# Attention, soft mixture of experts and a Mish layer in one kernel: the small products that build the next slice of the combined weight, placed one unit earlier

## The chip, the cores and the metric

The kernel runs on one core of one Trainium2 chip. The metric is the device time of one execution in microseconds (us). A core has five engines, each with its own instruction queue: TensorE (PE, with its weight loads shown apart as PEld), VectorE (DVE), ScalarE (ACT), GpSimd (POOL) and SyncE (SP, which issues the DMAs here).

## The reference

Three layers follow each other. `phi`, `w1`, `w2`, `w_in` and `w_out` are parameters, and all is in 32-bit floating point.

```python
q_rot, k_rot = (rotate(q), rotate(k))                 # (4, 8, 576, 64)
attn = softmax(1/sqrt(D) * q_rot @ k_rot.T)
x = (attn @ v) laid out as (2304, 512)

logits = x @ phi                                      # 8 experts x 4 slots
d = softmax(logits, axis=0); slot_input = (d.T @ x).reshape(E, 4, 512)
slot_out[e] = np.maximum(slot_input[e] @ w1[e], 0.0) @ w2[e]
x = softmax(logits, axis=1) @ slot_out                # rank 32

h = x @ w_in                                          # (2304, 2048)
g = h * np.tanh(softplus(h))                          # mish
return g @ w_out                                      # (2304, 512)
```

## The kernel before

The kernel has three stages: attention (to about 390 us of the span), the expert products, and from about 439 us on the Mish layer. The change lies in the Mish layer alone.

**The Mish layer.** Since x is the softmax `c` (2304 x 32) times `slot_out` (32 x 512), h = c @ (slot_out @ w_in). The kernel first builds the combined weight W = slot_out @ w_in in `wst` (2048 columns), and then takes c.T (`ct`) through it. Work goes in *units*: unit u is a block of 256 tokens (index i) against a slice j of 256 of the 2048 columns. There are 9 token blocks in three groups g of three, and 8 slices. In each group, for each slice j in turn, come three units, one per token block; these three are a *step* below. The first group (units 0 to 23) also builds W and the parts of w_out; the other two groups reuse them.

For a unit, `mish(u)` (L1000 to L1009) does two matmuls of 256 columns into the PSUM tile `hp`, the Mish activation on ACT into `gg`, and a rounded copy `gh`. `rest(u)` (L1015) takes the rest `gl` = gg - gh on DVE. `second(u)` (L1034) does twelve matmuls of 512 columns into the output tiles `o_ps`: gh times `wo_h`, gh times `wo_l`, and, last, gl times `wo_h`. It runs one unit behind: PE does hp of unit u, then the second product of unit u - 1.

**Inner products.** Slice j of W comes from two small products. `inner_a(j)` (L977, L978) does four matmuls of `s_t` with a block of w_in into the PSUM tile `m_wp`, which ACT copies. `inner_b(j)` (L983 to L986) does one matmul of that copy into `m_w`; ACT copies it into `wst`, and DVE takes the rest of rows 64 to 127 there by a subtraction. hp of slice j reads the result of that subtraction. `hp`, `m_wp` and `m_w` share two PSUM buffers.

```python
def inner_b(j):
    ps = ps_p.tile([128, 256], F32, tag="p", name="m_w")
    pin(nc.tensor.matmul(ps, lhsT=rr, rhs=wps[j % 2], start=True, stop=True))
    dst = wst[:, j * 256:(j + 1) * 256]
    pin(nc.scalar.copy(dst, ps))
    pin(nc.vector.tensor_tensor(out=dst[64:128], in0=ps[64:128], in1=dst[64:128].bitcast(F32), op=ALU.subtract))
```

**Chunks of w_out.** w_out comes in 16 chunks of 128 rows, each as a rounded part `wo_h` and a rest `wo_l`; slice j needs chunks 2j and 2j + 1. Chunks 0 to 3 were prepared earlier and lie in `wo_l`; `parts_of(c)` splits one, with a copy on ACT (L940) and a subtraction on DVE (L941). Chunks 4 to 15 are loaded raw and converted in small steps: two scale operations on ACT (L871, L872), five on DVE (L874, L876, L879, L881, L883), then a copy on ACT (L885) and a last subtraction on DVE (L887). `convert(n)` emits the next n DVE steps of this stream, with the ACT operations among them; a raw load (L863) goes out from within it. Each unit calls it with 3, the first unit of a step with 4.

**Order.** `pin` keeps all these instructions in the order of the code, so each engine's queue is the order in which the loop over units calls these functions:

```python
for u in range(len(units) + 2):
    ...
        mish(u)
        if u == 0:
            convert(3)
            idle(5)
        else:
            if u in (1, 2):
                parts_of(u + 1)
            if g == 0 or u == NG * GR:
                rest(u - 1)
                convert(3 + (i == 0))
            ...
    if u >= lag and u != NG * GR:
        second(u - lag)
    ...
    if g == 0 and j + 1 < NG:
        if i == 1:
            inner_a(j + 1)
        elif i == 2:
            inner_b(j + 1)
```

So within step j, m_wp of the next slice follows the second product in unit i = 1, and m_w follows it in unit i = 2, right ahead of hp of the next step. Ahead of the loop stand `inner_a(0)`, `inner_b(0)`, `parts_of(0)` and `parts_of(1)`; `idle(n)` puts n matmuls of no use (`warm`) on PE. In the trace `room` is the name of several work tiles (gg, raw chunks, copies of m_wp).

Of the kernel before, what the change touches and what calls it, by code (L numbers as in the profile page):

```python
# [42 lines left out]
def kernel(  # L43
# [78 lines left out]
    def fetch(key, behind=False):  # L122
        m, e, hf = key
        t = parts[key][0]
        if m == 3:
            lds = [(t.rearrange("p (c f) -> p c f", c=KDM), scr_in[e])]
        else:
            w = (w1, w2)[m - 1]
            n = w.shape[1] // 2
            lds = [(t.rearrange("p (c f) -> p c f", c=n // 128),  # L130
                    w[e, hf * n:(hf + 1) * n, :].rearrange("(c p) f -> p c f", p=128))]
            if (m, e // 4, hf) == (2, E // 4 - 1, 1):

                final.append(lds.pop())
                if len(final) == 4:
                    lds = [(o[:, c], i[:, c]) for c in range(n // 128) for o, i in final]
        for out, in_ in lds:
            ld = nc.sync.dma_start(out=out, in_=in_)
            if behind:
                tc.keep_in_program_order(ld)  # L140
# [724 lines left out]
    def cv(c, k):  # L865

        lo, hi = words(raws[c % 4])
        w = ws3[c % 3]
        wb, sf = w.bitcast(U32), sg.bitcast(F32)
        if k == "S":  # L870
            pin(nc.scalar.activation(out=hi.bitcast(F32), in_=hi.bitcast(F32), func=AF.Copy, scale=2.0 ** -112))  # L871
            pin(nc.scalar.activation(out=lo.bitcast(F32), in_=lo, func=AF.Copy, scale=2.0 ** -52))  # L872
        elif k == 1:
            pin(nc.vector.tensor_scalar(out=sg, in0=hi, scalar1=0x80000000, scalar2=None, op0=ALU.bitwise_and))  # L874
        elif k == 2:
            pin(nc.vector.scalar_tensor_tensor(out=wb, in0=hi, scalar=3, in1=sg, op0=ALU.logical_shift_left,  # L876
                                               op1=ALU.bitwise_or))
        elif k == 3:
            pin(nc.vector.tensor_scalar(out=sg, in0=wb, scalar1=0xFF800000, scalar2=None, op0=ALU.bitwise_and))  # L879
        elif k == 4:  # L880
            pin(nc.vector.tensor_tensor(out=sf, in0=sf, in1=lo.bitcast(F32), op=ALU.mult))  # L881
        elif k == 5:
            pin(nc.vector.tensor_tensor(out=w, in0=w, in1=sf, op=ALU.add))  # L883
        elif k == "H":
            pin(nc.scalar.copy(wo_h[c], w))  # L885
        else:
            pin(nc.vector.tensor_tensor(out=wo_l[c], in0=w, in1=wo_h[c].bitcast(F32), op=ALU.subtract))  # L887
# [49 lines left out]
    def parts_of(c):  # L937

        x = wo_l[c].bitcast(F32)
        pin(nc.scalar.copy(wo_h[c], x))  # L940
        pin(nc.vector.tensor_tensor(out=wo_l[c], in0=x, in1=wo_h[c].bitcast(F32), op=ALU.subtract))  # L941
# [21 lines left out]
    def convert(n):  # L963
        while n:
            x = next(steps2, None)
            if x is None:
                return
            cv(*x)
            n -= x[1] not in ("S", "H")

    def inner_a(j):

        fb, o = divmod(j * 256, 512)
        wi = parts[3, fb, 0][0].rearrange("p (c f) -> p c f", c=KDM)[:, :, o:o + 256]
        ps = ps_p.tile([128, 256], F32, tag="p", name="m_wp")
        for c in range(KDM):
            pin(nc.tensor.matmul(ps[32 * c:32 * c + 32, :], lhsT=s_t[:, c, :], rhs=wi[:, c, :], start=True, stop=True))  # L977
        pin(nc.scalar.copy(wps[j % 2], ps))  # L978
# [8 lines that stand above are left out]
# [8 lines left out]
    def mish(u):  # L995
        i, j = units[u]
        hp = ps_p.tile([128, 2, 256], F32, tag="p", name="hp")
        for x in range(2):
            f = 2 * j + x
            pin(nc.tensor.matmul(hp[:, x, :], lhsT=wst[:, f * 128:(f + 1) * 128],  # L1000
                                 rhs=ct[:, i * 256:(i + 1) * 256],
                                 start=True, stop=True))
        hp = hp.rearrange("p a n -> p (a n)")
        gg = ggs[u % 3]
        gh = p6.tile([128, 512], F32R, tag="gh", name="gh", bufs=LOOK + 1)
        gl = p6.tile([128, 512], F32R, tag="gl", name="gl", bufs=LOOK + 1)
        pin(nc.scalar.activation(out=gg, in_=hp, func=AF.Mish))  # L1007

        pin((nc.scalar.copy if 0 < u < NG * GR else nc.vector.tensor_copy)(gh, gg))  # L1009
        gs[u] = gh, gl, gg  # L1010

    def rest(u):

        gh, gl, gg = gs[u]
        pin(nc.vector.tensor_tensor(out=gl, in0=gg, in1=gh.bitcast(F32), op=ALU.subtract))  # L1015
        gs[u] = gh, gl
# [3 lines left out]
    def second(u):  # L1020
        i, j = units[u]
        gh, gl = gs.pop(u)
        todo = [(n, x, k) for n in range(2) for x in range(2) for k in range(3)]
        if u < NG * GR:

            todo.sort(key=lambda y: y[2] == 2)
        if j == 0:
            for n in range(2):
                ops[i, n] = ps_o.tile([128, DM], F32, tag="o", name="o_ps")
        for at, (n, x, k) in enumerate(todo):  # L1030
            g_, w_ = ((gh, wo_h), (gh, wo_l), (gl, wo_h))[k]
            f = 2 * j + x
            cols = slice(x * 256 + n * 128, x * 256 + n * 128 + 128)
            pin(nc.tensor.matmul(ops[i, n], lhsT=g_[:, cols], rhs=w_[f], start=(j == 0 and (x, k) == (0, 0)),  # L1034
                                 stop=(j == NG - 1 and all(y[0] != n for y in todo[at + 1:]))))
            if j == NG - 1 and all(y[0] != n for y in todo[at + 1:]):
                ob = obs[(2 * i + n) % 4]
                pin((nc.scalar.copy if n else nc.vector.tensor_copy)(ob, ops.pop((i, n))))
                store(2 * i + n, ob)
# [17 lines left out]
    def idle(n):  # L1057

        warm(ps_o, "o", n)
# [8 lines left out]
    for u in range(len(units) + 2):  # L1068

        lag = 1 if u < NG * GR else 2  # L1070
        if u < len(units):
            g, j = units[u][0] // GR, units[u][1]
            i = units[u][0] % GR
            mish(u)
            if u == 0:
                convert(3)
                idle(5)
            else:
                if u in (1, 2):
                    parts_of(u + 1)  # L1080
                if g == 0 or u == NG * GR:
                    rest(u - 1)
                    convert(3 + (i == 0))
                if g:
                    rest(u)
        else:
            g = None
        if u >= lag and u != NG * GR:
            second(u - lag)
        if g == 0 and i == 2 and j in (0, 2):  # L1090
            fetch((3, 2 + j // 2, 0), behind=True)
        if g == 0 and j + 1 < NG:
            if i == 1:
                inner_a(j + 1)
            elif i == 2:
                inner_b(j + 1)
    ring.close()

# [49 lines left out]
```

## Time and profile before

| | us |
|---|---|
| median of 3 runs (lowest to highest) | 682.52 (682.22 to 687.17) |
| the profiled execution | 684.97 |
| its span, first to last instruction | 683.2 |
| PE busy in the span | 629.7 (92%) |
| DVE busy | 408.0 (60%) |
| ACT busy | 337.2 (49%) |
| POOL busy | 216.9 (32%) |

The profile is one execution, taken by the hardware profiler. A timeline row gives the start from the span's beginning, the duration, the engine, the line of the code, the operation, what it writes and reads, and how many were merged (x2); in square brackets stands how long the engine had been idle before it and what ended that. Matmuls overlap each other, so the difference of two starts says more than a duration. Engines run side by side: idle time of one that is not the slowest costs nothing.

### The profile page before, as it was taken

Reading aid. Unit: us, or ns where it says so; the run is one execution under the profiler, and the core shown is the slowest. Engines: PE = TensorE matmul, PEld = TensorE weight load, DVE = VectorE, ACT = ScalarE, POOL = GpSimd, SP = SyncE. Lnnn points to the kernel's source line nnn. Section 1 sums busy time; section 2 is a strip of 40 time slices with the busy share of each in tenths; the row PEclk is TensorE's granted clock in tenths of the full one; section 3 lists DMA queues with packets and bytes.
Section 4 is the critical chain, followed back from the end, with each engine's and each line's share of the span. In section 5 each row is a group of like instructions: output and inputs, shape, how many; then the busy total and the mean of one; then the engine's idle time right before and its main releaser. Section 6 shows DMA issues by size and latency. Waiting matters only on the chain.

```text
span 683.2 us, 11115 instructions
## 1 busy us (share of the span) xinstructions
PE 629.7 (92%) x4034; PEld 463.2 (68%) x4034; DVE 408.0 (60%) x824; ACT 337.2 (49%) x757; POOL 216.9 (32%) x263
## 2 busy tenths in 40 slices
PE   1698899987899999999999898988989999999997
PEld 1566677665676677677667664456767888888885
DVE  6677688787687865656565533276766533343332
ACT  2565676684687656655566312265655311221121
POOL 6668768754968545424300010000000000000000
PEclk9999999999999999999999999999999999999999
DMA  8778589777886975436559579943200300030003
GB/s 258 185 181 223 167 269 265 227 208 226 198 245 210 280 201 144 106 96 167 133 182 321 191 248 379 402 165 138 78 32 2 92 1 0 1 93 0 1 1 93
DMA packets 59607, 109.43 MB, mean 160 GB/s; under 512 B 12832, under 2 KB 25248, under 8 KB 59040
## 3 DMA queue, kind: packets, MB, share of 16 engines
q1 hardware_dynamic: 59552, 108.72, 53.4%
q8 instruction: 32, 0.52, 0.3%
q14 instruction: 23, 0.19, 0.1%
HBM read 70.25 MB, written 9.96 MB: 117 GB/s over the span
## 4 chain that ended last, share of the span: by engine, by line
PE 76%; DMA 9%; DVE 6%; ACT 3%; POOL 2%; issue 1%; SPq 1%; ACTq 0%; DVEq 0%; POOLq 0%
PE o_ps L1034 29%; PE m_av L429 13%; PE t L374 7%; PE s L333 5%; PE s L335 4%; DMA w<-in_moe_w_in_dram 3%; PE hp L1000 3%; PE so_ps L896 2%; PE s L353 2%; DMA w<-in_moe_w_dram 2%; PE m_lg L455 1%; DVE nmax L361 1%; PE warm L553 1%; ACT P L367 1%; PE tk L388 1%
## 5 line engine op out<-in xcount | busy, mean ns | idle before, releaser
L361 DVE TENSOR_REDUCE nmax<-s 128x1 f32<-128x576 f32 x144 | 108.0, 752 | 64.6 <-PE s L335 41.6
L367 ACT ACTIVATE P<-s,nmax 128x576 f32<-128x576 f32 x144 | 107.2, 745 | 37.9 <-DVE nmax L361 26.1
L1034 PE MATMUL o_ps<-wo_h,gh 128*128 128x512 f32 x288 | 113.1, 393 | 0.1
L1034 PE MATMUL o_ps<-wo_l,gh 128*128 128x512 f32 x288 | 113.0, 392 | 0.0
L1034 PE MATMUL o_ps<-wo_h,gl 128*128 128x512 f32 x288 | 100.9, 391 | 2.3 <-DVE gl L1015 2.3
L1007 ACT ACTIVATE room<-hp 128x512 f32<-128x512 f32 x72 | 43.0, 599 | 112.2 <-PE hp L1000 107.5
L333 PE MATMUL s<-qk_st 128*128 128x288 f32 x256 | 86.0, 351 | 11.9 <-ACT P L367 6.0
L374 PE MATMUL t<-cs,P 128*128 128x128 f32 x512 | 79.4, 283 | 4.8 <-ACT P L367 2.7
L410 ACT COPY PT<-t 128x512 f32<-128x512 f32 x92 | 53.5, 586 | 49.5 <-PE t L374 48.8
L429 PE MATMUL m_av<-PT,w 128*64 128x320 f32 (+1 forms) x384 | 73.9, 422 | 3.2 <-DVE PT L413 1.9
L374 PEld LDWEIGHTS t<-cs,P 128*128 128x128 f32 x512 | 59.9, 143 | 22.1 <-issue 10.2
L335 PE MATMUL s<-k_st,qk_st 128*128 128x288 f32 x256 | 74.1, 303 | 0.0
L333 PEld LDWEIGHTS s<-qk_st 128*128 128x128 f32 x256 | 50.1, 196 | 32.0 <-ACT P L367 10.4
L1009 DVE CAST gh<-room 128x512 fp32r<-128x512 f32 x49 | 20.9, 427 | 79.1 <-ACT room L1007 78.9
L1034 PEld LDWEIGHTS o_ps<-wo_h,gl 128*128 128x128 f32 x288 | 53.9, 188 | 14.9 <-DVE gl L1015 3.5
L231 POOL TENSOR_TENSOR w<-w,cs 128x512 f32<-128x512 f32 x34 | 45.2, 1330 | 55.0 <-PE m_k L285 45.1
L1034 PEld LDWEIGHTS o_ps<-wo_h,gh 128*128 128x128 f32 x288 | 54.1, 188 | 9.6 <-DVE gh L1009 0.3
L1034 PEld LDWEIGHTS o_ps<-wo_l,gh 128*128 128x128 f32 x288 | 54.4, 189 | 8.9
L1015 DVE TENSOR_TENSOR gl<-room,gh 128x512 fp32r<-128x512 f32 x72 | 49.6, 690 | 5.0 <-DVE gh L1009 0.5
L335 PEld LDWEIGHTS s<-k_st,qk_st 128*128 128x128 f32 x256 | 50.5, 197 | 0.0
L228 POOL TENSOR_TENSOR w<-w,cs 128x512 f32<-128x512 f32 x34 | 45.1, 1326 | 9.0 <-DMA w<-in_k_dram 4.8
L429 PEld LDWEIGHTS m_av<-PT,w 128*64 128x64 f32 x384 | 26.6, 136 | 24.3 <-issue 9.3
(175 smaller groups left out, 1014.1 us busy)
## 6 DMA issues: line engine op xcount, KB each, us to landing
w<-in_moe_w_dram SPq DMA_DIRECT2D x28, 1024.0 KB, 7.5
w<-in_moe_w_in_dram SPq DMA_DIRECT2D x16, 512.0 KB, 7.7
qk_st<-parth SPq DMA_DIRECT2D x46, 144.0 KB, 3.2
qk_st<-partl SPq DMA_DIRECT2D x46, 144.0 KB, 3.3
room<-in_moe_w_out_dram SPq DMA_DIRECT2D x12, 512.0 KB, 3.5
w<-in_q_dram SPq DMA_DIRECT2D x16, 256.0 KB, 5.5
w<-in_k_dram SPq DMA_DIRECT2D x16, 256.0 KB, 5.1
w<-in_moe_w_dram SPq DMA_DIRECT2D x16, 256.0 KB, 5.9
```

The costliest lines, as they stand in the source:

```text
L228: eng.tensor_tensor(out=tb, in0=src, in1=sin.to_broadcast([128, n, w]), op=ALU.mult)
L231: eng.tensor_tensor(out=dst, in0=sv, in1=cv, op=ALU.mult)
L333: nc.tensor.matmul(s[:, half, 0:288], lhsT=st[:, qc:qc + 128], rhs=st[:, KC + o:KC + o + 288], start=first, stop=False)
L335: nc.tensor.matmul(s[:, half, 0:288], lhsT=st[:, qc:qc + 128], rhs=k2_st[p % 2][:, o:o + 288], start=False, stop=last)
L361: nc.vector.tensor_reduce(out=stat[p][0][:, i:i + 1], in_=s[:, :, 0:288], axis=AX.XY, op=ALU.max, negate=True)
L367: nc.scalar.activation(out=P[p, t][:, h * S:(h + 1) * S].rearrange("p (a b) -> p a b", a=2), in_=s[:, :, 0:288], func=AF.Exp, bias=stat[p] ...
L374: nc.tensor.transpose(ps[:, j, :], P[p, t][:, blk * 128:(blk + 1) * 128], ident)
L410: nc.scalar.copy(dst, src)
L429: nc.tensor.matmul(ps[o:o + 64, :], lhsT=lhsT, rhs=rhs, start=(c == 0), stop=(c == 4))
L1007: pin(nc.scalar.activation(out=gg, in_=hp, func=AF.Mish))
L1015: pin(nc.vector.tensor_tensor(out=gl, in0=gg, in1=gh.bitcast(F32), op=ALU.subtract))
L1034: pin(nc.tensor.matmul(ops[i, n], lhsT=g_[:, cols], rhs=w_[f], start=(j == 0 and (x, k) == (0, 0)), stop=(j == NG - 1 and all(y[0] != n fo ...
```

## The change

The inner products move one unit ahead: inner_a(j + 1) goes behind the second product of the step's first unit (i = 0), inner_b(j + 1) behind that of its second (i = 1). In unit 0, where there is no second product yet, inner_a(1) follows the `idle` matmuls. Further, parts_of(2), which stood ahead of rest(0) in unit 1, and parts_of(3), which stood ahead of rest(1) in unit 2, both go into unit 1, right behind rest(0).

```diff
@@ -1076,10 +1076,11 @@
                 convert(3)
                 idle(5)
             else:
-                if u in (1, 2):
-                    parts_of(u + 1)
                 if g == 0 or u == NG * GR:
                     rest(u - 1)
+                    if u == 1:
+                        parts_of(2)
+                        parts_of(3)
                     convert(3 + (i == 0))
                 if g:
                     rest(u)
@@ -1090,9 +1091,10 @@
         if g == 0 and j + 1 < NG:
-            if i == 1:
+
+            if i == 0:
                 inner_a(j + 1)
-            elif i == 2:
+            elif i == 1:
                 inner_b(j + 1)
```

On PE, at the start of the loop, before: the matmuls hp of unit 0, the useless ones, hp of unit 1 and the second product of unit 0.

```order
1262 L1000 MATMUL hp<-ct,wst 128x256 x2
1263 L553 MATMUL warm<-cs 128x128 x5
1264 L1000 MATMUL hp<-ct,wst 128x256 x2
1265 L1034 MATMUL o_ps<-wo_h_4888,gh 128x512
1266 L1034 MATMUL o_ps<-wo_l_4904,gh 128x512
```

The same place on PE after the change:

```order
1262 L1000 MATMUL hp<-ct,wst 128x256 x2
1263 L553 MATMUL warm<-cs 128x128 x5
1264 L977 MATMUL m_wp<-w_0_0_4767,s_t 32x256 x4
1265 L1000 MATMUL hp<-ct,wst 128x256 x2
1266 L1034 MATMUL o_ps<-wo_h_4888,gh 128x512
```

m_wp of slice 1 now stands ahead of hp of unit 1; before, it came behind the second product of unit 0.

On DVE, in units 1 and 2, before (L941 is the subtraction of parts_of, its tile number 4906 that of chunk 2 and 4907 of chunk 3; L1015 is gl; the rest are conversion steps):

```order
579 L879 TENSOR_SCALAR room<-room 128x512
580 L941 TENSOR_TENSOR wo_l_4906<-wo_l_4906,wo_h_4890 128x512
581 L1015 TENSOR_TENSOR gl<-room,gh 128x512
582 L881 TENSOR_TENSOR room<-room 128x512
583 L883 TENSOR_TENSOR room<-room 128x512
584 L874 TENSOR_SCALAR room<-room 128x512
585 L941 TENSOR_TENSOR wo_l_4907<-wo_l_4907,wo_h_4891 128x512
586 L1015 TENSOR_TENSOR gl<-room,gh 128x512
```

The same place on DVE after the change (L986 is the subtraction of inner_b):

```order
579 L879 TENSOR_SCALAR room<-room 128x512
580 L1015 TENSOR_TENSOR gl<-room,gh 128x512
581 L941 TENSOR_TENSOR wo_l_4906<-wo_l_4906,wo_h_4890 128x512
582 L941 TENSOR_TENSOR wo_l_4907<-wo_l_4907,wo_h_4891 128x512
583 L881 TENSOR_TENSOR room<-room 128x512
584 L883 TENSOR_TENSOR room<-room 128x512
585 L874 TENSOR_SCALAR room<-room 128x512
586 L986 TENSOR_TENSOR wst<-m_w,wst 64x256
587 L1015 TENSOR_TENSOR gl<-room,gh 128x512
```

gl of unit 0 now comes ahead of both chunks' parts; gl of unit 1 has both of them, three conversion steps and the subtraction for slice 1 ahead of it.

On ACT, in the step that follows, after the change (L978 copies m_wp, L985 copies m_w, L1007 is Mish, L1009 gh; L871 and L872 are the scale operations, L885 the copy of a converted chunk):

```order
428 L978 COPY room<-m_wp 128x256
429 L1007 ACTIVATE room<-hp 128x512
430 L1009 CAST gh<-room 128x512
431 L871 ACTIVATE room<-room 128x512
432 L872 ACTIVATE room<-room 128x512
433 L985 CAST wst<-m_w 128x256
434 L1007 ACTIVATE room<-hp 128x512
```

The copy of m_w now stands ahead of the Mish of the step's third unit; before, it stood ahead of that of the next step's first unit.

## Rows read from the trace of the kernel before

**Rows 1.** Busy us (instructions) of PE, PEld, DVE, ACT, POOL; clock, DMA, GB/s

```profile
450.00:480.00 30.00, 25.88 (x126) 19.32 (x125) 21.10 (x38) 18.58 (x35) 0.00 (x0) 1.00 0.41 151
```

**Rows 2.** Waits from 436 to 540 us: total us, times, longest

```profile
DVE wst L986 <- ACT wst L985: 14.6, 7, 3.2
...
PE hp L1000 <- DVE wst L986: 6.5, 7, 0.9
...
DVE wo_l L941 <- ACT wo_h L940: 4.2, 3, 2.3
...
PE o_ps L1034 <- DVE gl L1015: 2.3, 2, 1.4
```

**Rows 3.** Timeline, end of a step: start, duration, engine, line, [idle before <-releaser]

```profile
465.28 0.59 PE L983 MATMUL m_w<-room,cs 128*128 128x256 f32 x2
...
465.91 0.37 ACT L985 CAST wst<-m_w 128x256 fp32r<-128x256 f32 x1 [1.41 <-PE m_w L983]
466.31 0.43 DVE L986 TENSOR_TENSOR wst<-m_w,wst 64x256 fp32r<-64x256 f32 x1 [2.72 <-ACT wst L985]
466.77 0.69 DVE L1015 TENSOR_TENSOR gl<-room,gh 128x512 fp32r<-128x512 f32 x1
...
466.79 0.51 PE L1000 MATMUL hp<-ct,wst 128*128 128x256 f32 x2 [0.92 <-DVE wst L986]
...
468.95 1.07 PE L1034 MATMUL o_ps<-wo_h,gl 128*128 128x512 f32 x4
...
469.86 0.40 PE L1000 MATMUL hp<-ct,wst 128*128 128x256 f32 x2
```

**Rows 4.** Timeline of PE: two more starts of a step, and m_wp

```profile
455.44 0.50 PE L1000 MATMUL hp<-ct,wst 128*128 128x256 f32 x2 [0.92 <-DVE wst L986]
...
461.61 0.64 PE L977 MATMUL m_wp<-w,s_t 128*32 128x256 f32 x8
...
462.18 0.51 PE L1000 MATMUL hp<-ct,wst 128*128 128x256 f32 x2
...
523.43 0.50 PE L1000 MATMUL hp<-ct,wst 128*128 128x256 f32 x2 [0.93 <-DVE wst L986]
```

**Rows 5.** Timeline of the stage's start, 440 to 449 us

```profile
440.79 0.60 PE L983 MATMUL m_w<-room,cs 128*128 128x256 f32 x2
...
441.22 1.50 PE L553 MATMUL warm<-cs 128*128 128x128 f32 x12
...
443.83 0.48 PE L1000 MATMUL hp<-ct,wst 128*128 128x256 f32 x2
...
444.35 0.60 ACT L1007 ACTIVATE room<-hp 128x512 f32<-128x512 f32 x1 [0.42 <-PE hp L1000]
...
444.98 0.62 ACT L1009 CAST gh<-room 128x512 fp32r<-128x512 f32 x1
...
445.51 0.61 ACT L940 CAST wo_h<-wo_l 128x512 fp32r<-128x512 f32 x1
...
446.15 0.69 DVE L941 TENSOR_TENSOR wo_l<-wo_l,wo_h 128x512 fp32r<-128x512 f32 x1 [0.24 <-ACT wo_h L940]
...
446.76 0.68 DVE L1015 TENSOR_TENSOR gl<-room,gh 128x512 fp32r<-128x512 f32 x1
447.37 0.68 DVE L881 TENSOR_TENSOR room<-room 128x512 f32<-128x512 f32 x1
...
447.50 1.20 PE L1034 MATMUL o_ps<-wo_h,gl 128*128 128x512 f32 x4 [0.95 <-DVE gl L1015]
448.08 0.69 DVE L883 TENSOR_TENSOR room<-room 128x512 f32<-128x512 f32 x1
...
448.87 0.43 DVE L874 TENSOR_SCALAR room<-room 128x512 uint32<-128x512 uint32 x1
```

**Rows 6.** Timeline, the last converted part and its matmul

```profile
526.12 0.69 DVE L887 TENSOR_TENSOR wo_l<-room,wo_h 128x512 fp32r<-128x512 f32 x1 [0.69 <-ACT wo_h L885]
...
527.45 0.40 PE L1034 MATMUL o_ps<-wo_l,gh 128*128 128x512 f32 x1
```

## The prediction

> **What bounds the kernel now.** I read the busy time by stretch first, then who waits for whom in the last stage, then the timeline of one step and of the stage's start. The change touches only the first 24 units of the last stage, from about 439 to 533 us of the span. In a piece of that stretch [rows 1] the reader is to see that TensorE (PE) is busy 25.88 of 30 us at a granted clock of 1.00, the upper of its two levels (2.4 GHz), while VectorE (DVE) has 21.10 us of work, ScalarE (ACT) 18.58, and GpSimd none. So PE sets the pace there and does not quite fill it. The list of waits [rows 2] says what it waits for: seven times, 6.5 us in all, the first matmul of a unit (hp) waits for the subtraction that finishes a slice of wst, and twice, 2.3 us in all, a second product (o_ps) waits for gl.
>
> The timeline of one step's end [rows 3] shows the first wait whole. PE does m_w at 465.28, ACT copies it at 465.91, DVE subtracts at 466.31, and hp, which is PE's very next instruction and reads that slice, starts at 466.79. Nothing lies between m_w and hp that could cover the round trip through ACT and DVE. The steps repeat this: hp at 455.44, 466.79 and, five steps on, 523.43 [rows 3, 4], so one step takes (523.43 - 466.79) / 5 = 11.33 us.
>
> **The change part by part.** No instruction is added or removed; one group goes a unit earlier, and four small instructions change places at the start. SP's queue is the same, since the loads of raw chunks are issued from the conversion steps, whose number per unit stays.
>
> *Steady steps.* With m_w a unit earlier, the hp behind it belongs to the third unit of the same step and reads an old slice. The hp that needs the new slice comes a whole unit later. A unit from hp to hp takes 469.86 - 466.79 = 3.07 us [rows 3]; the round trip takes 466.79 - 465.28 = 1.51. It is covered. What stays is m_w itself: at the stage's start, where no dependency follows, the next matmul begins 441.22 - 440.79 = 0.43 us after m_w [rows 5]. So hp starts 1.51 - 0.43 = 1.08 us earlier per step, and there are seven. The idle time that the trace prints before this hp is only 0.92 [rows 4], counted from m_w's end, and 7 x 0.92 = 6.4 would be the sum by it. I take the starts, 7 x 1.08 = 7.6. The Trainium skill (Perfetto Trace Analysis, Tensor Engine Instruction) says that the profiler computes the end of a TensorE instruction rather than observing it, which favours counting from starts; the list of waits alone would give the smaller sum.
>
> m_wp (0.57 us from its first matmul to hp [rows 4]) and its copy also move by one unit. It keeps a whole second product between itself and m_w, as before, so its own cost is unchanged in these steps. Its weights are loaded well ahead.
>
> What is late next is gl. DVE works in order, and the subtraction waits there: it sat idle 2.72 us for it in this step with gl queued behind it, which then starts at 466.77 [rows 3]. That is 1.49 us after m_w's start; PE could take a gl 0.74 us after gl starts (446.76 to 447.50 [rows 5]), so 2.23 us after m_w. PE will want it 0.43 us later than m_w (hp) plus 468.95 - 466.79 = 2.16 [rows 3], at 2.59. So 0.36 us are left, against 0.92 more before. Enough, if ACT and DVE come to the copy and the subtraction on time. DVE's idle time before the subtraction is 14.6 us over seven steps [rows 2], 2.1 each. The step shortens by 1.08, so some 1.0 is left and DVE still arrives first. The Trainium skill (the same page and section) calls ScalarE and VectorE strictly first in, first out; that rule speaks against the change, since gl of the second unit can't pass a subtraction that now stands ahead of it. The trace agrees (2.72 us idle with gl behind), and what it would cost is the first rival below.
>
> *Start of the stage* [rows 5]. Before, hp of unit 1 starts at 443.83, PE waits 0.95 us for gl of unit 0 until 447.50, then up to 1.4 for gl of unit 1 [rows 2], then the first 1.08. I walk it anew:
> - m_wp now stands before hp of unit 1: 443.83 + 0.57 = 444.40.
> - gl of unit 0 is wanted 2.16 later, at 446.56. DVE was free at 446.15 - 0.24 = 445.91, and gl now goes first there: usable at 445.91 + 0.74 = 446.65. The wait is 0.09, no longer 0.95.
> - The gl matmuls take 469.86 - 468.95 = 0.91, so m_w is at 447.56, hp of unit 2 at 447.99, and gl of unit 1 is wanted at 450.15.
> - ACT: the first mish of unit 1 comes 444.35 - 443.83 = 0.52 after hp, at 444.92; gh 0.63 later at 445.55; the first copy (wo_h) 0.53 later at 446.08. DVE's part of that chunk follows 446.15 - 445.51 = 0.64 behind, at 446.72. The second part is 0.61 later (447.33), then two steps of 0.61 and 0.71 (447.94, 448.65), then a step 0.79 later at 449.44 with 0.43 of its own, then the subtraction at 449.87, and 466.77 - 466.31 = 0.46 later gl of unit 1, at 450.33. PE can use it at 451.07, a wait of 0.92.
> - Hence hp of unit 3 at 451.07 + 0.91 = 451.98, where it was at 455.44 [rows 4]: 3.46 us earlier, the first 1.08 among them.
>
> So moving the parts of two chunks behind gl is worth 0.86 at unit 0, and having both in DVE's queue ahead of gl of unit 1 gives up little, because that gl also waited before.
>
> *End of the stretch* [rows 6]. The last converted part ends at 526.12 + 0.69 = 526.81 and its matmul, the fourth of its product, starts at 527.45: 0.64 to spare. Behind the last subtraction DVE now has one more gl, two steps and a lo part, 0.61 + 0.71 + 0.43 + 0.61 = 2.36 by rows 5, and PE one more unit (3.07) but 1.08 less of wait: 0.64 + 3.07 - 2.36 - 1.08 = 0.27. I take no wait; it could cost some tenths, once.
>
> **Sum.** 3.46 + 6 x 1.08 = 9.9 us. The profiled execution took 684.97 us with a span of 683.2, so it would take 675.0. The median of the runs shown is 682.52, 2.45 below that one execution, and the forecast goes from the median: 682.52 - 9.9 = 672.6. Bounds: with idle times by ends, 3.46 - 0.16 + 6 x 0.92 = 8.8 (673.7). With no wait at all for gl of unit 1 (0.92 more), 671.7; a PE that restarts less often may save 0.1 more per step, 671.0.
>
> **The rivals.**
> 1. *The wait goes over to gl.* For: only 0.36 us to spare; on ACT two scale instructions come to stand right ahead of the copy of m_w. Against: ACT was idle 11 us in 30 [rows 1] and waited 1.41 for m_w in this step [rows 3]. If every step lost 0.6, the gain would be 9.9 - 7 x 0.6 = 5.7: 676.8.
> 2. *The start gives nothing but its share of the round trip*, because both chunks' parts ahead of gl of unit 1 cost what gl of unit 0 gains (0.61 + 0.64 of DVE and ACT against 0.86, and m_wp's 0.57 no longer hidden). Then 7 x 1.08 = 7.6: 674.9. For: gl of unit 1 is already the late one. Against: the walk above.
> 3. *Nothing changes*: PE is held elsewhere and each 1.08 comes back as another wait, for gl or for gh: 682.5. Against: nothing else in the list of waits [rows 2] belongs to PE in these steps.
> 4. *Slower.* DVE falls behind and reaches the subtraction late in every step, with gl behind it. The place is the chain by which a converted chunk goes DVE to ACT (copy wo_h) and back, on which DVE waits 2.3 us at worst [rows 2]. DVE has 1.0 us to spare per step, and PE 0.36 more for gl. From 1.0 + 0.36 + 9.9 / 7 = 2.8 us lost per step on it is slower than before; with 2.3 and one more copy and its way to DVE ahead of it (0.53 + 0.64 [rows 5], so 3.5), 7 x 0.7 = 5 us slower: 687.5. For: DVE's order in each step changes. Against: its work per step, 0.7 of the time, doesn't.
>
> **How the numbers follow.** The forecast has 0.68, rival 1 0.12, rival 2 0.10, rival 3 0.05 and rival 4 0.05. A measurement of this kernel can tell about 1% from no change; 1% is 6.8 us, so 675.7. The forecast and rival 2 are faster by more, as is a third of rival 1: 0.82. The rest of rival 1 and rival 3 are within it: 0.13. Slower has 0.05. The range goes from 670.8 (the lower bounds above) to 677.0, which takes in rivals 1 and 2.
>
> **What would show it right or wrong.** In the changed profile hp should no longer appear among the waits for wst; the step from hp to hp should be 10.2 to 10.3 us; the wait for gl of unit 0 should be near 0.1 and that of unit 1 near 0.9; the stage's later units should be unchanged. Waits of o_ps for gl in every step would mean rival 1, DVE waiting long for wo_h rival 4. A step of 11.3 us with other waits makes the prediction wrong, as does hp of unit 3 no earlier than 3 us before its old place.

## The result and the profile after

| | before | after |
|---|---|---|
| median, us (12 runs each, lowest to highest) | 685.49 (682.22 to 689.66) | 675.06 (672.80 to 681.14) |
| ratio, 95% interval | | 0.9855 (0.9827 to 0.9884) |
| the profiled execution | 684.97 | 673.89 |
| its span | 683.2 | 672.1 |

The changed kernel is faster by 1.45% (1.2 to 1.7), 9.9 us of 685.49. The time forecast was 672.6 with a range of 670.8 to 677.0 and a chance of 0.82 for faster by over 1%.

The same stretch as [rows 1], by busy time of each engine, in the changed kernel (columns as there):

```profile
450.00:480.00 30.00, 29.43 (x152) 22.98 (x153) 23.38 (x42) 20.05 (x37) 0.00 (x0) 1.00 0.46 169
```

PE is now busy 29.43 us of 30, where it was 25.88. DVE and ACT do more in the same 30 us, since the same work is packed closer.

The list of waits of the changed kernel from 436 to 530 us (total us, times, longest), beside [rows 2]:

```profile
DVE wst L986 <- ACT wst L985: 10.9, 6, 2.2
...
PE o_ps L1034 <- DVE gl L1015: 0.9, 1, 0.9
...
DVE wo_l L887 <- ACT wo_h L885: 0.7, 1, 0.7
...
DVE wo_l L941 <- ACT wo_h L940: 0.4, 1, 0.4
```

The wait of hp for wst is gone from the list. Of the two waits of o_ps for gl one is left. DVE still waits for the copy of m_w, 10.9 us in six steps, so it still comes first to that place.

The timeline of the changed kernel: the stage's start, beside [rows 5], then one step, beside [rows 3], and the end of the stretch, beside [rows 6].

```profile
443.30 0.64 PE L977 MATMUL m_wp<-w,s_t 128*32 128x256 f32 x8
...
443.87 0.50 PE L1000 MATMUL hp<-ct,wst 128*128 128x256 f32 x2
...
445.13 0.68 DVE L1015 TENSOR_TENSOR gl<-room,gh 128x512 fp32r<-128x512 f32 x1
...
446.06 1.09 PE L1034 MATMUL o_ps<-wo_h,gl 128*128 128x512 f32 x4
446.21 1.29 DVE L941 TENSOR_TENSOR wo_l<-wo_l,wo_h 128x512 fp32r<-128x512 f32 x2 [0.40 <-ACT wo_h L940]
...
446.99 0.59 PE L983 MATMUL m_w<-room,cs 128*128 128x256 f32 x2
...
449.04 0.39 PE L1034 MATMUL o_ps<-wo_h,gh 128*128 128x512 f32 x1
...
449.27 0.39 PE L1034 MATMUL o_ps<-wo_l,gh 128*128 128x512 f32 x1
449.38 0.43 DVE L986 TENSOR_TENSOR wst<-m_w,wst 64x256 fp32r<-64x256 f32 x1
449.82 0.69 DVE L1015 TENSOR_TENSOR gl<-room,gh 128x512 fp32r<-128x512 f32 x1
...
450.57 1.19 PE L1034 MATMUL o_ps<-wo_h,gl 128*128 128x512 f32 x4 [0.91 <-DVE gl L1015]
...
451.60 0.40 PE L1000 MATMUL hp<-ct,wst 128*128 128x256 f32 x2
...
458.32 0.59 PE L983 MATMUL m_w<-room,cs 128*128 128x256 f32 x2
...
458.56 0.59 PE L1000 MATMUL hp<-ct,wst 128*128 128x256 f32 x2
...
458.95 0.37 ACT L985 CAST wst<-m_w 128x256 fp32r<-128x256 f32 x1 [0.79 <-PE m_w L983]
458.98 0.39 PE L1034 MATMUL o_ps<-wo_h,gh 128*128 128x512 f32 x1
...
459.21 0.61 ACT L1007 ACTIVATE room<-hp 128x512 f32<-128x512 f32 x1
...
459.35 0.43 DVE L986 TENSOR_TENSOR wst<-m_w,wst 64x256 fp32r<-64x256 f32 x1 [1.86 <-ACT wst L985]
...
459.79 0.69 DVE L1015 TENSOR_TENSOR gl<-room,gh 128x512 fp32r<-128x512 f32 x1
...
460.60 0.87 PEld L1034 LDWEIGHTS o_ps<-wo_h,gl 128*128 128x128 f32 x4
460.82 1.07 PE L1034 MATMUL o_ps<-wo_h,gl 128*128 128x512 f32 x4
...
461.73 0.40 PE L1000 MATMUL hp<-ct,wst 128*128 128x256 f32 x2
...
512.46 0.40 PE L1000 MATMUL hp<-ct,wst 128*128 128x256 f32 x2
...
515.51 0.69 DVE L887 TENSOR_TENSOR wo_l<-room,wo_h 128x512 fp32r<-128x512 f32 x1 [0.69 <-ACT wo_h L885]
...
516.26 0.19 PEld L1034 LDWEIGHTS o_ps<-wo_l,gh 128*128 128x128 f32 x1 [0.17 <-DVE wo_l L887]
```

In the step, hp follows m_w without idle time in brackets, and the copy and the subtraction run beside the second product that comes next. The hp that needs the slice starts at 461.73, and the subtraction ended at 459.78. At the start, gl of unit 0 comes before the two parts and PE takes it at 446.06 without a wait; gl of unit 1 is late, by 0.91 as the trace prints it. At the end, the last chunk's part finishes at 516.20, just as its weights are to be loaded.

To compare traces I count from the first m_wp of the stage, since what lies before it varies from execution to execution (last section). Three numbers describe a kernel: hp of unit 3, hp of unit 21 (the last step of the first group), and the step between, (hp of 21 - hp of 6) / 5, all from each kernel's timeline of PE. For the kernels that were not timed there is the profiled execution alone.

| kernel | hp of unit 3 | step | hp of unit 21 | earlier than before | timed ratio, 95% interval |
|---|---|---|---|---|---|
| before | 16.00 | 11.33 | 83.99 | | |
| after | 12.86 | 10.15 | 73.72 | 10.27 | 0.9855 (0.9827 to 0.9884) |
| inner products only | 14.96 | 10.15 | 75.85 | 8.14 | 0.9872 (0.9843 to 0.9900) |
| parts only | 13.46 | 11.35 | 81.53 | 2.46 | 0.9975 (0.9956 to 0.9993) |
| no round trip | 14.71 | 10.19 | 75.82 | 8.17 | 0.9900 (0.9870 to 0.9930) |
| parts in unit 2 | 11.68 | 10.15 | 73.50 | 10.49 | 0.9864 (0.9822 to 0.9906) |
| one copy more | 12.87 | 10.43 | 75.42 | 8.57 | not timed |
| three copies more | 12.88 | 11.21 | 80.13 | 3.86 | not timed |
| parts split | 12.26 | 10.15 | 73.16 | 10.83 | not timed |
| spread | 11.74 | 10.15 | 72.64 | 11.35 | 0.9827 (0.9773 to 0.9881) |

### The profile page after: what moved, and what is told of

Same layout as the page of the kernel before. It is cut to its first block, busy times and chain, and to the rows that moved or that the text cites. A ratio compares the mean times of both kernels' runs of the same rounds, so it can differ in the third digit from the quotient of the medians.

```text
span 672.1 us, 11113 instructions
## 1 busy us (share of the span) xinstructions
PE 626.1 (93%) x4034; PEld 462.7 (69%) x4034; DVE 407.8 (61%) x824; ACT 335.9 (50%) x757; POOL 217.1 (32%) x263
## 4 chain that ended last, share of the span: by engine, by line
PE 77%; DVE 8%; DMA 7%; ACT 3%; issue 2%; SPq 1%; POOL 1%; DVEq 0%; ACTq 0%; POOLq 0%
PE o_ps L1034 29%; PE m_av L429 12%; PE t L374 7%; PE s L333 5%; DMA w<-in_moe_w_in_dram 4%; PE s L335 4%; PE hp L1000 3%; PE s L353 2%; PE h_ps L830 2%; PE so_ps L896 2%; DVE nmax L361 2%; PE m_lg L455 1%; ACT P L367 1%; PE warm L553 1%; PE tk L388 1%
## 5 line engine op out<-in xcount | busy, mean ns | idle before, releaser
L1007 ACT ACTIVATE room<-hp 128x512 f32<-128x512 f32 x72 | 43.0, 599 | 106.7 <-PE hp L1000 102.2
L374 PEld LDWEIGHTS t<-cs,P 128*128 128x128 f32 x512 | 59.5, 143 | 22.3 <-issue 10.9
L1009 DVE CAST gh<-room 128x512 fp32r<-128x512 f32 x49 | 20.9, 427 | 79.4 <-ACT room L1007 79.3
L1015 DVE TENSOR_TENSOR gl<-room,gh 128x512 fp32r<-128x512 f32 x72 | 49.6, 691 | 4.6
```

The costliest lines, as they stand in the source:

```text
L374: nc.tensor.transpose(ps[:, j, :], P[p, t][:, blk * 128:(blk + 1) * 128], ident)
```

## The experiments

**Inner products only.** Against the changed kernel:

```diff
+                if u in (1, 2):
+                    parts_of(u + 1)
                 if g == 0 or u == NG * GR:
                     rest(u - 1)
-                    if u == 1:
-                        parts_of(2)
-                        parts_of(3)
```

> The inner products moved as in the change, the parts of chunks 2 and 3 left where they were. Theory (the round trip from m_w to hp is what the steps lose): the step from hp to hp is 10.1 to 10.2 us as in the changed kernel, not 11.33; but at the start gl of unit 0 stands behind a part that waits for a later copy, so the waits for gl of units 0 and 1 are about 1.5 us each, and hp of unit 3 comes 14.5 to 15.2 us after the first m_wp (before 16.00, changed 12.86). In all 7.5 to 8.5 us faster than before. Rival (the parts make the gain): steps of 11.3 us and no more than 2 us faster.

Measured: steps of 10.15, hp of unit 3 at 14.96, and 675.2 us (median) against 684.7, ratio 0.9872. The two waits for gl stay (1.34 and 1.39, expected about 1.5 each), as PE's rows of the timeline show:

```profile
446.86 1.20 PE L1034 MATMUL o_ps<-wo_h,gl 128*128 128x512 f32 x4 [1.34 <-DVE gl L1015]
...
451.95 1.20 PE L1034 MATMUL o_ps<-wo_h,gl 128*128 128x512 f32 x4 [1.39 <-DVE gl L1015]
```

What the steps gain comes from the inner products alone.

**Parts only.** Against the kernel before:

```diff
-                if u in (1, 2):
-                    parts_of(u + 1)
                 if g == 0 or u == NG * GR:
                     rest(u - 1)
+                    if u == 1:
+                        parts_of(2)
+                        parts_of(3)
```

> Only the parts of chunks 2 and 3 moved behind gl of unit 0, the inner products as before. Theory: steps of 11.3 us with the wait of hp for wst in each (0.92 by the trace); the waits for gl shrink from 2.3 us to 0.5 or less; hp of unit 3 about 13.7 us after the first m_wp; 2 to 2.5 us faster than before. With the first run the two parts should add up to the whole, 10 us. Rival (the parts make the gain): 7 us or more faster.

Measured: 682.68 us against 684.7, ratio 0.9975; hp of unit 3 at 13.46, no matmul of o_ps that waits for gl in the first group, and the step unchanged (11.35), with its old wait in the list of waits:

```profile
PE hp L1000 <- DVE wst L986: 6.5, 7, 0.9
```

Alone, the parts bring 2.46 us within the stage and the inner products 8.14; together 10.27, not 10.60. What is missing is in the start: up to hp of unit 3 the two alone bring 2.54 and 1.04, together 3.14 and not 3.58, for with both PE gets to gl of unit 1 earlier and has to wait for it.

**No round trip.** The kernel before, its order untouched:

```diff
-            f = 2 * j + x
+            f = 2 * (j - (j > 0 and u < NG * GR and i == 0)) + x
             pin(nc.tensor.matmul(hp[:, x, :], lhsT=wst[:, f * 128:(f + 1) * 128],
             ...
```

> The kernel before in its order, but hp of the first unit of each step in the first group reads the slice of the step before, which is long done, so that hp does not depend on the m_w right ahead of it (these units then compute with the wrong slice). Theory: the dependency alone costs the time, so the step falls to 10.1 to 10.3 us with no move at all, hp of unit 3 comes 14.8 to 15.0 us after the first m_wp, and it is 7.5 to 8.5 us faster than before. Rival (PE is held by something else in the step, and the move helps by other means, such as the shared PSUM buffers or the queue of DVE): the step stays over 11 us and other waits take its place.

Measured: the step falls to 10.19 us with no instruction moved (four of the six steps take 10.15 to 10.17, the longest 10.29), hp of unit 3 is at 14.71, and 677.12 us against 684.7, ratio 0.9900. The shared PSUM buffers and the order on every engine were as before, so what the steps lost was the dependency of hp on the m_w right ahead of it. Both waits for gl at the start stay (0.92 and 1.35). New waits appear at the end, for the last chunk:

```profile
519.49 0.19 PEld L1034 LDWEIGHTS o_ps<-wo_h,gh 128*128 128x128 f32 x1 [0.38 <-ACT wo_h L885]
...
520.22 0.50 PE L1034 MATMUL o_ps<-wo_l,gh 128*128 128x512 f32 x1 [0.23 <-DVE wo_l L887]
```

There the last chunk's parts come late: with PE faster, the conversion in its old order has no more time to spare. Unit 22 takes 522.39 - 518.68 = 3.71 us from hp to hp, where before it took 2.98, and from hp of unit 21 to the end of the span it is 160.59 us, 0.8 more than before (159.77). So the 8.17 of the table overstates this run: from the first m_wp to the end it gains 7.35 us, below the 7.5 to 8.5 expected, which fits its smaller timed gain.

**Parts in unit 2.** Against the changed kernel:

```diff
-                    if u == 1:
+                    if u == 2:
                         parts_of(2)
                         parts_of(3)
```

> The changed kernel, but the parts of chunks 2 and 3 both go behind gl of unit 1, in unit 2. Theory (the 0.9 us wait for gl of unit 1 comes from the two parts in DVE's queue ahead of it, and a DVE that has too much to do in units 1 to 3 only passes the wait on): no wait for gl of unit 1, but one of 0.5 to 1.0 us for gl of unit 2; hp of unit 3 some 0.8 us earlier than in the changed kernel, hp of unit 6 within 0.3 us of it. Same time as the changed kernel within 0.5 us. Rival (the wait is a matter of place alone): no wait for any gl, 0.9 us faster than the changed kernel.

Measured: hp of unit 3 at 11.68, 1.18 earlier than after the change (0.8 expected), and hp of unit 6 at 22.77 against 22.99. Most of the wait had moved to the next gl:

```profile
456.40 1.20 PE L1034 MATMUL o_ps<-wo_h,gl 128*128 128x512 f32 x4 [0.68 <-DVE gl L1015]
```

The time is that of the changed kernel (675.12 against 675.06). Moving the parts as a pair moves the wait and takes 0.22 off the stage (73.50 against 73.72).

**One copy more, three copies more.** The changed kernel, with ACT's copy of m_w repeated (n = 1 and n = 3):

```diff
-        pin(nc.scalar.copy(dst, ps))
+        for _ in range(n + 1 if j else 1):
+            pin(nc.scalar.copy(dst, ps))
```

> The changed kernel, but ACT copies m_w into wst twice (the same values), for slices 1 to 7, which makes the way from m_w to gl of the second unit longer by one copy, 0.26 to 0.40 us. Theory (after the change 0.29 us are left between the moment gl can be used and the moment PE wants it: in one step of its trace gl starts 1.47 after m_w, usable 0.74 later, wanted at 2.50): steps of 10.15 to 10.30 us, with waits of o_ps for gl of at most 0.15. Rival 1 of the prediction in its sharp form (the wait has moved to gl and nothing is left): steps of 10.4 to 10.55 us.

> As the run before, but with three further copies (the way from m_w to gl longer by 0.8 to 1.2 us). Theory: what goes past the 0.29 us left comes back in full as a wait of o_ps for gl in each step: steps of 10.65 to 11.05 us, 0.5 to 0.9 more than the changed kernel's 10.15. Rival (the result is due only a unit later, when hp reads it, and ACT and DVE have idle time, so a longer way is free): steps of 10.15 us.

Measured: steps of 10.43 and 11.21 us. The timeline of the second, whose line numbers from L985 on are higher by one:

```profile
459.76 0.59 PE L983 MATMUL m_w<-room,cs 128*128 128x256 f32 x2
...
460.39 1.58 ACT L986 CAST wst<-m_w 128x256 fp32r<-128x256 f32 x4 [0.79 <-PE m_w L983]
...
462.01 0.43 DVE L987 TENSOR_TENSOR wst<-m_w,wst 64x256 fp32r<-64x256 f32 x1 [3.07 <-ACT wst L986]
...
463.20 0.97 PE L1035 MATMUL o_ps<-wo_h,gl 128*128 128x512 f32 x3 [0.77 <-DVE gl L1016]
...
464.23 0.40 PE L1001 MATMUL hp<-ct,wst 128*128 128x256 f32 x2
```

Four copies take 1.58 us where one takes 0.37, so a further one is 0.40. Three lengthen the way by 1.21 and the step by 11.21 - 10.15 = 1.06, more than the 0.5 to 0.9 expected. One lengthens the way by 0.40 and the step by 0.28, which is outside my range (steps of 10.15 to 10.30) and inside that of the rival (10.4 to 10.55). So the idea that the longer way is free falls, and the step has less to spare than my 0.29 us: by these differences 0.12 to 0.15.

The starts show where the rest goes. In the second run the matmuls of gl start 463.20 - 459.76 = 3.44 us after m_w, in the changed kernel 460.82 - 458.32 = 2.50. That is 0.94 later, or 1.21 less 0.27, so up to this start my 0.29 held. The other 0.12 comes behind it: the matmuls of a gl that was late take 464.23 - 463.20 = 1.03 to the next hp, those of one in time 461.73 - 460.82 = 0.91. In the first run the list of waits has no such wait of a matmul in the steps, but the load of gl as PE's weights waits in each:

```profile
461.18 0.59 PE L983 MATMUL m_w<-room,cs 128*128 128x256 f32 x2
...
463.80 0.77 PEld L1035 LDWEIGHTS o_ps<-wo_h,gl 128*128 128x128 f32 x4 [0.38 <-DVE gl L1016]
463.81 1.20 PE L1035 MATMUL o_ps<-wo_h,gl 128*128 128x512 f32 x4
...
464.84 0.40 PE L1001 MATMUL hp<-ct,wst 128*128 128x256 f32 x2
```

Its matmuls start 463.81 - 461.18 = 2.63 after m_w, 0.13 later than in the changed kernel, and again take 1.03 to hp. In the changed kernel this load starts 0.22 ahead of its matmul, at 460.60, and gl, usable at 459.79 + 0.74 = 460.53, is in time for it by no more than 0.07.

**Parts split, and spread.** Against the changed kernel, the first line for both and the second for "spread":

```diff
-                    if u == 1:
-                        parts_of(2)
-                        parts_of(3)
-                    convert(3 + (i == 0))
+                    if u in (1, 2):
+                        parts_of(u + 1)
+                    convert(3 + (i == 0) - (u in (1, 2)) + (u in (7, 8)))
```

In "parts split" the call of `convert` stays as it was.

> The changed kernel, but only the part of chunk 2 goes behind gl of unit 0 (unit 1), and that of chunk 3 behind gl of unit 1 (unit 2). Theory: one DVE subtraction less (0.61 us) ahead of gl of unit 1, so its wait falls from 0.91 to about 0.3, and gl of unit 2 waits 0.1 to 0.3; hp of unit 21 comes 0.3 to 0.6 us earlier after the first m_wp than the changed kernel's 73.72. Rival (whatever leaves the one gl is waited for in full at the next, as in the run with both parts in unit 2): within 0.15 us of 73.7.

> As the run before, and one conversion step less in each of units 1 and 2, one more in each of units 7 and 8. Theory (the waits that are left come from DVE having more to do in units 1 to 3 than PE's time there, and later DVE has about 1 us to spare per step): no wait for gl at all, hp of unit 3 near 12.0, steps of 10.15 us, hp of unit 21 near 72.9 after the first m_wp, so 0.8 us faster than the changed kernel, and no wait for the last chunk's parts over 0.3 us. Rival (the conversion is late by then): waits for wo_h or wo_l in units 6 to 9 or at the end that take the 0.8 us back.

Measured: "parts split" leaves one wait, 0.35 us for gl of unit 1, none for gl of unit 2, where I had expected 0.1 to 0.3, and brings hp of unit 21 to 73.16. "Spread" has no matmul that waits for gl in the first group (two loads of weights wait, 0.6 us in all); hp of units 3 and 6 follow each other as in a steady step:

```profile
450.21 0.39 PE L1000 MATMUL hp<-ct,wst 128*128 128x256 f32 x2
...
460.38 0.40 PE L1000 MATMUL hp<-ct,wst 128*128 128x256 f32 x2
```

Its hp of unit 21 is at 72.64, 1.08 us before that of the changed kernel. The timed median, 673.11 us (ratio 0.9827), is the lowest of all, but its interval holds the changed kernel's ratio: by the times alone the two can't be told apart, by the traces the stage is 1.08 us shorter.

## Why the prediction was right

The forecast of the gain was 9.9 us. The medians differ by 10.4, the ratio says 9.9, and within the stage the traces differ by 10.27 up to hp of unit 21. The two profiled executions differ by 11.1; 0.70 of that lies before the stage (first m_wp at 439.44 and 438.74) and has nothing to do with the change. The absolute time came out 2.5 us above the forecast, because the forecast started from the median of three runs, 682.52; over twelve it was 685.49. Within the gain two errors of opposite sign met: the steps from hp of unit 3 to hp of unit 21 gave 7.13 us where the sum has 6 x 1.08 = 6.48, the start 3.14 where it has 3.46. The mechanism came out as forecast; that the sum came this close is in part luck.

- *The steady steps.* Forecast 1.08 us each by differences of starts; the step fell by 11.33 - 10.15 = 1.18. The idle time printed before hp, 0.92, would have been short by a fifth. The 0.1 above the forecast lies in hp itself. This is the matmul behind hp in the step of [rows 3], before:

```profile
467.13 0.40 PE L1034 MATMUL o_ps<-wo_h,gh 128*128 128x512 f32 x1
```

From m_w to this matmul it takes 467.13 - 465.28 = 1.85 before and 458.98 - 458.32 = 0.66 after, 1.19 less. The hp that had waited takes 467.13 - 466.79 = 0.34 of it; after, 0.66 less the 0.43 of m_w [rows 5] leaves 0.23. This is the restart of PE that the prediction named as a bound and did not put into the sum. That the printed idle time is short the rows show too: m_w ends after 0.59 or 0.60 by the trace, yet the next matmul starts 0.43 after it [rows 5]. The Trainium skill (Perfetto Trace Analysis, Tensor Engine Instruction) says that a matmul's end is an estimate in the profile; these rows fit that, but can't tell it from an overlap of two matmuls.

- *That it is the round trip, and nothing else in the step*, is shown by the run without the dependency: the same step, to 0.04, with no move. Rival 3 (nothing changes) falls with it and with the step of the changed kernel.
- *The start.* Forecast 3.46 us earlier for hp of unit 3, measured 16.00 - 12.86 = 3.14. The waits came in the places walked: none for gl of unit 0 (0.09 forecast), one for gl of unit 1. That the trace prints 0.91 for it, where the walk had 0.92, is chance: the walk counts from starts, and by starts gl of unit 1 was wanted at 449.27 + 0.23 = 449.50 (0.23 from one of these matmuls to the next) and taken at 450.57, 1.07 later. The 0.32 that is missing: hp of unit 1 came 5.13 after the first m_wp, not 4.39 + 0.57 = 4.96, for m_wp starts at 4.56 behind the useless matmuls, where hp had started at 4.39. ACT and DVE pass this 0.17 on, and gl of unit 1 starts at 449.82, 11.08 after the first m_wp, not 450.33 - 439.44 = 10.89. And from the start of the late gl matmuls to hp it takes 451.60 - 450.57 = 1.03, not 0.91. The rest is 0.03. In the run with the parts in unit 2, where this wait is gone, hp of unit 3 comes 1.18 earlier, about 1.07 + 0.12.
- *Rival 2* (the start gives only its share of the round trip) falls by the run with the parts alone: 2.46 us.
- *Rival 1* (gl takes over the wait) did not happen, but it was nearer than I said. I worked out 0.36 us to spare; the trace shows 2.50 - 1.47 - 0.74 = 0.29, for the 2.16 from hp to gl that I used was that of an hp that had waited. The runs with longer ways show 0.12 to 0.15, since a gl that comes too late costs 0.12 beside its delay (1.03 against 0.91), which the prediction left out. In the run with three copies more, DVE is idle for 3.07 us in front of the subtraction, and gl starts only behind it, at 462.45, though gh of its unit was done at 458.46. The Trainium skill (Perfetto Trace Analysis, Tensor Engine Instruction) states that VectorE's queue is strictly first in, first out; the trace agrees.
- *The end.* Of the 0.27 us that I thought were left, nothing was: the last part ends at 516.20 and its weight load waits until 516.26. Unit 22 takes 518.45 - 515.44 = 3.01 us from hp to hp, 2.98 before, so it costs 0.03 here; in the run without the dependency it costs some 0.7. The prediction had allowed for "some tenths, once".
- *Rival 4* (DVE behind) left no trace: its longest wait for wo_h in the loop is 0.7 us, where it was 2.3.

## What to carry to other kernels

Where a matmul reads what two other engines make of the matmul right before it, one independent unit of work between them hides the whole round trip, if the unit lasts longer (here 3.07 us against 1.51); what it is worth is the difference of two starts, with the dependency and without, times the number of rounds. Take the second start at the matmul behind the one that waits, since that one takes longer too (here by 0.11). After such a move look for the instruction that now stands behind the moved wait in an in-order queue, and test how much is left by lengthening the chain by a known amount. Look at the weight loads too: here one waited 0.38 us where no matmul did. Here a start-up wait that came from too much work in a few units was not removed by moving the work one unit, but by spreading it over units that had time.

## What the runs showed beside that

- The stage in question repeats closely: the six steps of the changed kernel from hp of unit 3 to hp of unit 21 take 10.13 to 10.15 us, and from hp of unit 21 to the end of the span it is 159.77 us before, 159.64 after and 159.69 with the parts in unit 2. What comes before the stage does not repeat: the first m_wp starts between 438.03 and 441.81 us in ten profiled executions. Already the last m_q product of the attention stage starts at 353.9 us in one (inner products only) and 357.7 in another (parts in unit 2), where the two programs are the same. What sets it apart was not looked into. Differences under 2 us are therefore read from the stage and not from the times.
- A repeated copy of ACT to the same place costs 0.40 us a piece, while the Mish of the next unit starts 0.26 us after a single copy of 0.37 (458.95 to 459.21 in the timeline of the changed kernel).
